# Pooled attention and a ReLU² feed-forward: the first batch pooled on VectorE, the second by accumulating transfers, two hidden blocks begun early

## The chip, the cores and the metric

The kernel runs on one core of a Trainium2 chip. A time is the device time of one execution in microseconds (us). The kernel before has a median of 930.41 us over three runs (928.98 to 931.21).

Engines are called as in the profile: PE is TensorE, DVE VectorE, ACT ScalarE, POOL GpSimd, SP SyncE. SP issues the plain transfers; POOL issues those that add to what lies in the destination ("sums" below).

## The reference, cut to what matters

```python
# q, k, v: [8 batches, 8 heads, 576 tokens, 64]; pool = 8, Sp = 72
k_p = k.reshape(B, H, Sp, pool, D).mean(axis=3)
v_p = v.reshape(B, H, Sp, pool, D).mean(axis=3)
scores = scale * np.matmul(q, k_p.transpose(0, 1, 3, 2))
scores = scores - np.max(scores, axis=-1, keepdims=True)
attn = np.exp(scores)
attn = attn / (np.sum(attn, axis=-1, keepdims=True) + 1e-09)
x = np.matmul(attn, v_p)              # as rows: [4608, 512]
h = np.maximum(x @ w_in, 0.0)         # w_in [512, 2048]
out = h * h @ w_out                   # w_out [2048, 512]
```

## The kernel before, in words

The 4608 token rows are cut into nine chunks of 512. A chunk takes 16 steps, one for each 128 columns of w_in: a *hidden* block (`h`: x times w_in, 128 × 512), ReLU and square on ACT, and, three steps later (LAG), a *project* block (`o`: its product with the rows of w_out, four accumulators kept in PSUM over the chunk). Chunk 0 does both products in plain float32; chunk 1 uses a split in two float32r parts and three products; from chunk 2 on a scheme with seven products takes the place of eight. The attention of a later chunk is done between these blocks, one pair of heads at a time. A chunk has 512 rows and a batch 576, so chunk 1 needs the pooled keys and values of batches 0 and 1, chunk 2 those of batches 1 and 2.

Every engine works strictly in the order in which the code was written. A table `work` says by `at(step, f, ...)` in which step a piece is written; within a step the order is fixed by the loop at the end of the kernel.

The front is the part ahead of step 0: the attention of chunk 0, written out by hand. For every pair of heads it has these stages: pooled keys and the queries are turned by PE (`turn_k`, tile `kps`; `turn_rows`, tile `qps`) and copied by ACT (`kf`, `st`); scores (`token_scores`, tile `sps`), row maximum on DVE (`tm`), exponent on ACT (`te`), division on DVE (`token_normalise`), turned back by PE (`token_turn`, tile `pps`) and copied (`sc`), weighed with the pooled values (`weigh_values`, tile `av`) and copied (`x`). `keep_awake` puts a few idle matmuls (`still`) in front of some of these.

Weights arrive as raw 512 KB tiles (`land`; EAGER = 8 of them are asked for in the front) and are brought to float32 by two ACT instructions (`magnitude`) and three DVE instructions (`to_float32`) each; FIRST tiles are converted in the front, the others in the steps.

Pooling is done in two ways. Batches 0 and 1 arrive whole, a pair of heads to a tile (`load_pair`, 288 KB), and are halved three times by POOL (`by_halves`: three TENSOR_TENSOR per pair); two of the key pairs of batch 0 are reduced by DVE (`reduce_k`). From batch 2 on four heads go to a tile: one plain transfer of 144 KB lays down every eighth-row pair, three accumulating transfers of 144 KB each, issued by POOL, add the others, and `pool` adds the two halves on DVE. A batch has two such tiles for keys and two for values, so 12 accumulating transfers.

SP's transfers take turns on eight semaphores, so an issue waits for the transfer eight before it to land. `dynamic_dma_scratch_size=1024`, the room for POOL's transfers, is the same in both kernels.

Of the kernel before, what the change touches and what calls it, by code (L numbers as in the profile page):

```python
# [37 lines left out]
def pooled_attn_relu2_ffn(  # L38
# [21 lines left out]
    P = 128  # L60
# [18 lines left out]
    FIRST, EAGER, AHEAD = 2, 8, 3  # L79
# [177 lines left out]
    def load_sums(kind, b, n, j):  # L257

        if (kind, b) not in started:
            started.add((kind, b))  # L260
            if kind == "k":
                loaded["kq", b] = sb.tile([SP_, H, D], F32, name=f"kq_{b}", tag="kq", bufs=1)
        src = {"k": k, "v": v}[kind][b].rearrange("h (s j o) d -> j s h (o d)", j=POOL // 2, o=2)[j][:, n * HALF:(n + 1) * HALF]
        if j == 0:
            two[kind, n] = sb.tile([SP_, HALF, 2 * D], F32, name=f"{kind}2_{b}_{n}", tag="two", bufs=2)
            load(two[kind, n], src)
        else:
            GP.dma_start(two[kind, n], src, accum_op=ALU.add)
# [4 lines left out]
    def pool(kind, b, n):  # L273
        new_batch(b)
        dst = kv[b] if kind == "v" else loaded["kq", b]
        t = two.pop((kind, n))
        DVE.tensor_tensor(dst[:, n * HALF:(n + 1) * HALF], t[:, :, :D], t[:, :, D:], op=ALU.add)
        for p in range(n * NPAIR // 2, (n + 1) * NPAIR // 2):
            loaded["kp", b, p] = dst[:, 2 * p:2 * p + 2, :]

    def turn_k(b, pairs=range(NPAIR)):

        pairs = list(pairs)
        pt = (ps_a if b else ps_h).tile([P, 512], F32, name=f"kps_{b}_{pairs[0]}", tag="a" if b else "h")
# [12 lines left out]
        return then  # L297

    def split_k(b, src=None):
        src = kf[b] if src is None else src  # L300
        kh, kl = kk[b] = [sb.tile([P, NPAIR, 2, SP_], F32R, name=f"k{x}_{b}", tag=f"k{x}", bufs=2) for x in "hl"]
        for i, own, oth in heads:
            ACT.copy(kh[own, :, i, :], src[own])
            ACT.copy(kh[oth, :, i, :], src[own])
        for i, own, oth in heads:
            for rows in (own, oth):
                DVE.tensor_tensor(kl[rows, :, i, :], src[own], kh[own, :, i, :].bitcast(F32), op=ALU.subtract)
# [35 lines left out]
    def turn_rows(c, p):  # L343
        src = loaded.pop(("qn", c, p))
        st = live[c, p] = half_tile("s", f"st_{c}_{p}")
        for i, copy in enumerate((ACT.copy, DVE.tensor_copy if p > 1 else ACT.copy)):
            pt = ps_h.tile([P, 512], F32, name=f"qps_{c}_{p}_{i}", tag="h")
            for t in range(NTT):
                PE.transpose(pt[:D, t * P:(t + 1) * P], src[:, i, t, :], ident)
            copy(st[i * D:(i + 1) * D], pt[:D])  # L350
# [81 lines left out]
    def token_scores(c, p):  # L432
# [15 lines left out]
        def then():  # L448
            m = sb.tile([P, 4, 2, NTT], F32, name=f"tm_{c}_{p}", tag="tm", bufs=2)
            e = w_tile(F32, f"te_{c}_{p}")[:, :, :NTT * SP_].rearrange("p i (t n) -> p i t n", t=NTT)  # L450
            e = [e[:, i] for i in range(2)]
            for i in range(2):
                DVE.tensor_reduce(m[:, 0, i], views[i], axis=AX.X, op=ALU.max)
                DVE.tensor_scalar(m[:, 1, i], m[:, 0, i], -SCALE, None, op0=ALU.mult)
            for i in range(2):
                for t in range(NTT):
                    ACT.activation(e[i][:, t], views[i][:, t], AF.Exp, bias=m[:, 1, i, t:t + 1], scale=SCALE)
            live[c, p] = (e, m)
# [3 lines left out]
    def token_normalise(c, p):  # L462
        e, m = live[c, p]
        for i in range(2):
            DVE.tensor_reduce(m[:, 2, i], e[i], axis=AX.X, op=ALU.add)
        DVE.tensor_scalar(m[:, 3], m[:, 2], 1e-9, float(POOL), op0=ALU.add, op1=ALU.mult)
        DVE.reciprocal(m[:, 3], m[:, 3])
        for i in range(2):
            DVE.tensor_tensor(e[i], e[i], m[:, 3, i].unsqueeze(2).to_broadcast([P, NTT, SP_]), op=ALU.mult)
# [20 lines left out]
    def weigh_values(c, p):  # L490
# [4 lines left out]
        av = (ps_h if c < PLAIN else ps_a).tile([P, 512], F32, name=f"av_{c}_{p}", tag="h" if c < PLAIN else "a")  # L495
# [189 lines left out]
    GP.memset(still, 0.0)  # L685
# [55 lines left out]
    token_turn(0, 3)()
    weigh_values(0, 3)()

    for p in range(NPAIR):
        load_pair("k", 1, p)
    for p in range(NPAIR):
        load_pair("v", 1, p)
    issue_loads()
    for p in range(NPAIR):
# [139 lines left out]
```

## Time and profile before

| | us |
|---|---|
| median of three runs (lowest, highest) | 930.41 (928.98, 931.21) |
| the profiled execution, its own time | 927.71 |
| span from its first to its last instruction | 925.9 |
| PE busy / DVE / ACT / POOL | 902.9 / 560.1 / 512.3 / 416.6 |
| mean granted PE clock | 0.990 |

Busy time of PE is modelled from pipelined matmuls, so a PE that is shown busy can still be slowed by what feeds it. All arithmetic goes through one helper line (L34), so a group is known by its tiles, not by its line. In a row of the timeline the first number is the start, the second how long the merged piece lasted, and in brackets stands the idle time ahead of it with what ended it.

### The profile page before, as it was taken

How to read it: one execution, taken by the hardware profiler on the slowest of the kernel's cores; microseconds unless marked ns; L12 is line 12 of the kernel's file. 1: busy time of each engine (PE TensorE's matmuls, PEld its weight loads, DVE VectorE, ACT ScalarE, POOL GpSimd, SP SyncE). 2: the span in 40 equal slices, each digit the busy share in tenths (PEclk: the TensorE clock that was granted, in tenths of full speed). 3: DMA queues.
4: the chain of work that ended last, by engine and by line, in shares of the span. 5: the costliest groups of instructions: out<-in, count | busy, mean ns of one | idle time of the engine just before them, and what ended most of it. 6: DMA issues, size and time to landing. Idle time of an engine off the chain costs nothing.

```text
span 925.9 us, 14226 instructions
## 1 busy us (share of the span) xinstructions
PE 902.9 (98%) x5111; PEld 722.0 (78%) x5114; DVE 560.1 (60%) x971; ACT 512.3 (55%) x1021; POOL 416.6 (45%) x231
## 2 busy tenths in 40 slices
PE   6899999999998999999999999999999999999998
PEld 3444444577777888888888888888888888888987
DVE  3995887476778887555755575657644663353221
ACT  2677657466656655655565556555644564444343
POOL 4752225455544666565666656565444444200000
PEclk7999999999999999999999999999999999999999
DMA  9794655678645555765575557654433353345501
GB/s 253 211 268 95 144 162 155 155 211 223 178 100 162 141 137 118 198 142 135 131 194 137 134 143 182 145 134 127 160 115 115 116 160 104 125 149 178 209 1 46
DMA packets 154231, 138.72 MB, mean 150 GB/s; under 512 B 90360, under 2 KB 119032, under 8 KB 154160
## 3 DMA queue, kind: packets, MB, share of 16 engines
q1 hardware_dynamic: 125360, 127.13, 45.0%
q0 software_dynamic: 28800, 10.68, 10.0%
q8 instruction: 40, 0.66, 0.3%
q14 instruction: 31, 0.25, 0.1%
HBM read 119.65 MB, written 18.06 MB: 149 GB/s over the span
## 4 chain that ended last, share of the span: by engine, by line
PE 85%; DVE 7%; ACT 2%; issue 2%; DMA 2%; SPq 1%; POOL 0%; DVEq 0%; ACTq 0%
PE o L34 40%; PE h L34 37%; PE sps L34 4%; PE av L34 3%; DVE wf_i L34 1%; DVE tm L34 1%; DMA w_o<-kept 1%; DVE gl L34 1%; SPq L34 1%; ACT sc L34 1%; DVE xf L34 1%; DVE st L34 0%; DVE te L34 0%; ACT r L34 0%; DVE vp L34 0%
## 5 line engine op out<-in xcount | busy, mean ns | idle before, releaser
L34 PE MATMUL o<-w_o,gh 128*128 128x512 f32 x1024 | 322.2, 396 | 0.7 <-DMA w_o<-kept 0.5
L34 POOL PARTITION_ALL_REDUCE tot<-sc x56 | 188.8, 3420 | 83.2 <-issue 82.8
L34 PEld LDWEIGHTS o<-w_o,gh 128*128 128x128 f32 x1024 | 184.4, 188 | 45.3 <-issue 7.0
L34 PE MATMUL o<-w_o,gl 128*128 128x512 f32 x512 | 199.6, 390 | 0.0
L34 POOL PARTITION_ALL_REDUCE mx<-sc x56 | 109.3, 1996 | 63.0 <-ACT sc L34 60.7
L34 ACT ACTIVATE r<-h 128x512 f32<-128x512 f32 x144 | 83.5, 595 | 95.9 <-PE h L34 77.5
L34 PE MATMUL h<-x_T,w_S 128*128 128x256 f32 x1008 | 130.6, 283 | 3.6 <-ACT r L34 3.0
L34 PEld LDWEIGHTS h<-x_T,w_S 128*128 128x128 f32 x1008 | 125.1, 192 | 4.2 <-ACT r L34 3.2
L34 PEld LDWEIGHTS o<-w_o,gl 128*128 128x128 f32 x512 | 96.1, 188 | 21.3
L34 DVE TENSOR_TENSOR h<-h,u 128x256 f32<-128x256 f32 x168 | 72.7, 433 | 62.2 <-ACT u L34 33.1
L34 ACT COPY u<-h 128x256 f32<-128x256 f32 x112 | 41.7, 373 | 116.2 <-PE h L34 70.9
L34 PE MATMUL h<-x_B,w_A 128*128 128x256 f32 x672 | 98.5, 283 | 0.4 <-ACT r L34 0.4
L34 PEld LDWEIGHTS h<-x_B,w_A 128*128 128x128 f32 x672 | 91.9, 191 | 5.2 <-ACT r L34 0.8
L34 POOL DMA_DIRECT2D k<-in_k_dram x36 | 44.6, 1239 | 110.8 <-issue 56.2
L34 DVE TENSOR_TENSOR gl<-r,gh 128x512 fp32r<-128x512 f32 x128 | 90.3, 741 | 5.7 <-ACT gh L34 5.6
L34 POOL DMA_DIRECT2D v<-in_v_dram x36 | 44.0, 1223 | 107.1 <-issue 45.4
L34 DVE TENSOR_TENSOR u<-h,u 128x256 f32<-128x256 f32 x56 | 23.4, 418 | 107.9 <-ACT u L34 107.8
L34 ACT ACTIVATE r<-r 128x512 f32<-128x512 f32 x144 | 84.2, 625 | 1.1
L34 DVE TENSOR_TENSOR st<-qs,st 64x512 fp32r<-64x512 f32 x56 | 44.6, 797 | 60.1 <-ACT st L34 59.2
L34 ACT CAST gh<-r 128x512 fp32r<-128x512 f32 x128 | 78.9, 617 | 0.6 <-PE o L34 0.4
L34 ACT ACTIVATE sc<-sc 72x512 f32<-72x512 f32 x56 | 34.5, 632 | 67.0 <-DVE sc L34 67.0
L34 PE MATMUL h<-x,wf_i 128*128 128x512 f32 x128 | 59.4, 609 | 1.9 <-DVE wf_i L34 1.9
(96 smaller groups left out, 1224.1 us busy)
## 6 DMA issues: line engine op xcount, KB each, us to landing
w_o<-kept SPq DMA_DIRECT2D x128, 512.0 KB
out_dram<-ob SPq DMA_DIRECT2D x36, 256.0 KB
raw_i<-in_moe_w_in_dram SPq DMA_DIRECT2D x16, 512.0 KB
raw_o<-in_moe_w_out_dram SPq DMA_DIRECT2D x16, 512.0 KB
kept<-w_o SPq DMA_DIRECT2D x16, 512.0 KB
rb<-rd SPq DMA_DIRECT2D x56, 128.0 KB
k<-in_k_dram POOLq DMA_DIRECT2D x36, 144.0 KB, 5.0
v<-in_v_dram POOLq DMA_DIRECT2D x36, 144.0 KB, 5.3
```

The source lines that it names most:

```text
L34: return lambda *a, **k: self.tc.keep_in_program_order(f(*a, **k))
```

## The change

In the front of chunk 0: DVE reduces three key pairs of batch 0 and POOL one (before: two and two); POOL still halves the values of batch 0. Queries land a pair of heads at a time with the two heads side by side, so that one PE turn of 128 × 128 does both heads and one ACT copy follows (before: two turns of 64 × 128 and two copies). The scale and its sign go into the copy of the pooled keys (`kf`), so the maximum becomes a minimum and the extra multiplication goes. Normalising a pair is one reduction and one multiplication for both heads. Two hidden blocks are begun with each x as it arrives (`begin`). Four weight tiles are converted in the front. The idle tile is cleared by DVE.

Batch 1 arrives by accumulating transfers like the later batches: 4 plain ones of 144 KB and 12 sums. POOL's 24 TENSOR_TENSOR on batch 1 go. The sums of batch 1's keys stand in the front, those of its values in steps 0 to 2, and `pool` on DVE stands in step 2 (keys) and step 5 (values); the turn of batch 1's keys moves from step 1 to step 3. The transfers of batch 2 get a table of their own (NEXT_AT), and their keys are still turned in step 8.

```diff
-    FIRST, EAGER, AHEAD = 2, 8, 3
+    FIRST, EAGER, AHEAD = 4, 8, 3
-    EARLY = ((-15, -12, -10, -7), (0, 1, 2, 3, 4))
+    EARLY = ((-13, -12, -8, -7), (0, 1, 2, 3, 4))
+    NEXT_AT = {"k": ((3, 4, 5, 6, 7), (3, 4, 5, 6, 7)), "v": ((7, 8, 9, 11, 13), (7, 8, 10, 12, 14))}
-    STIR, AWAKE = 10, (2, 3, 3)
+    STIR, AWAKE = 10, (2, 2, 0)
...
-            ACT.copy(kf[b][:, pairs[0]:pairs[-1] + 1, :], turned)
+            ACT.activation(kf[b][:, pairs[0]:pairs[-1] + 1, :], turned, AF.Copy, scale=-SCALE)
...
-    def load_rows(c, j):
+    def load_rows(c, p):
-        t = w_tile(F32, f"qn_{c}_{j}")
...
+        rows = loaded["qn", c, p] = half_tile("qn", f"qn_{c}_{p}").rearrange("p (t h d) -> p t h d", t=NTT, h=2)
+        load(rows, q[0, 2 * p:2 * p + 2, c * CH:(c + 1) * CH, :].rearrange("h (p t) d -> p t h d", t=NTT))
...
+    def begin(cc):
+        for fc in range(2):
+            if cc == 0:
+                begun[fc] = ps_h.tile([P, 512], F32, name=f"h_0_{fc}", tag="h")
+            PE.matmul(begun[fc], lhsT=wf["i", 0, cc // 2, 0][:, cc % 2, fc * P:(fc + 1) * P], rhs=xts[0, cc][:, 0, :],
+                      start=cc == 0, stop=cc == NCC - 1)
...
+    for p in range(NPAIR):
+        load_pair("k", 0, p)
+        load_rows(0, p)
+    load_pair("v", 0, 0)
+    load_pair("v", 0, 1)
+    land(keys[0])
+    load_pair("v", 0, 2)
+    load_pair("v", 0, 3)
+    land(keys[1])
+    for n in range(2):
+        load_sums("k", 1, n, 0)
+    for key in keys[2:EAGER]:
         land(key)
+    for n in range(2):
+        load_sums("v", 1, n, 0)
...
+    for p in range(3):
+        reduce_k(0, p)
+    halve_k(0, 3)
+    more = [(n, j) for j in range(1, POOL // 2) for n in range(2)]
     for p in range(NPAIR):
         halve_v(0, p)
+        if p == 1:
+            load_sums("k", 1, *more.pop(0))
+    for n, j in more:
+        load_sums("k", 1, n, j)
...
-    for p in range(NPAIR):
-        halve_k(1, p)
-    for p in range(NPAIR):
-        halve_v(1, p)
-    at(1, turn_k, 1)
+    v_sums = [(n, j) for j in range(1, POOL // 2) for n in range(2)]
+    for i, (n, j) in enumerate(v_sums):
+        at(i // 2, load_sums, "v", 1, n, j)
+    for n in range(2):
+        at(2, pool, "k", 1, n)
+        at(5, pool, "v", 1, n)
+    at(3, turn_k, 1)
```

Three places show how the change moves instructions. In the names, `k_1` is a key tile of batch 1, `k_2` of batch 2, `v_0_3` the fourth value pair of batch 0; the last number is a buffer's.

POOL after the first value pairs of batch 0, before the change (its last value pair, the first of eight pairs of batch 1, and then, after the eighth, the first sums):

```order
L34 TENSOR_TENSOR v_0_3_86<-v_0_3_86 72x2x256
L34 TENSOR_TENSOR v_0_3_86<-v_0_3_86 72x2x128
L34 TENSOR_TENSOR vp_146<-v_0_3_86 72x128
L34 TENSOR_TENSOR k_1_0_462<-k_1_0_462 72x2x256
L34 TENSOR_TENSOR k_1_0_462<-k_1_0_462 72x2x128
L34 TENSOR_TENSOR kq_478<-k_1_0_462 72x128
```

and with the change (from the end of the second value pair):

```order
L34 TENSOR_TENSOR vp_158<-v_0_1_84 72x128
L34 DMA k_1_90<-in_k_dram 72x4x128
L34 TENSOR_TENSOR v_0_2_86<-v_0_2_86 72x2x256
L34 TENSOR_TENSOR v_0_2_86<-v_0_2_86 72x2x128
L34 TENSOR_TENSOR vp_158<-v_0_2_86 72x128
L34 TENSOR_TENSOR v_0_3_87<-v_0_3_87 72x2x256
L34 TENSOR_TENSOR v_0_3_87<-v_0_3_87 72x2x128
L34 TENSOR_TENSOR vp_158<-v_0_3_87 72x128
L34 DMA k_1_90<-in_k_dram 72x4x128 x5
L34 DMA v_1_97<-in_v_dram 72x4x128 x6
L34 DMA k_2_0_568<-in_k_dram 72x4x128
L34 DMA k_2_1_569<-in_k_dram 72x4x128
```

Twelve sums of batch 1 now stand ahead of batch 2's on the one queue of POOL, and the first of them stands ahead of two value pairs of batch 0.

PE around the turn of batch 1's keys, with the change (`h_3` is the fourth hidden block, `o_0` to `o_3` the four accumulators; the turn stood after `h_1` before):

```order
L34 MATMUL h_3_528<-x_3_428,wf_i_1_389 128x512
L34 MATMUL kps_0_533<-ident,kq_89 128x72 x4
L34 MATMUL o_0_538<-wf_o_440,r_0_459 128x512
L34 MATMUL o_1_539<-wf_o_440,r_0_459 128x512
L34 MATMUL o_2_540<-wf_o_440,r_0_459 128x512
L34 MATMUL o_3_541<-wf_o_440,r_0_459 128x512
L34 MATMUL h_4_572<-x_0_348,wf_i_0_449 128x512
```

All of PE's later work stands behind this turn.

DVE around the addition that ends the pooling of batch 1's keys (`kq`), with the change:

```order
L34 SCALAR_TENSOR_TENSOR wf_o_440<-raw_o_94,wf_o_440 128x512
L34 SCALAR_TENSOR_TENSOR wf_i_0_449<-raw_i_0_0_95,wf_i_0_449 128x2x256
L34 TENSOR_TENSOR kq_89<-k_1_90 72x256 x2
L34 TENSOR_SCALAR wf_i_1_473<-wf_i_1_473 128x2x256
L34 TENSOR_SCALAR wf_o_476<-wf_o_476 128x512
L34 SCALAR_TENSOR_TENSOR wf_i_1_473<-wf_i_1_473,raw_i_1_0_96 128x2x256
```

Half of the weights of block `h_4` (`wf_i_1_473`) are converted behind this addition; before the change POOL made `kq` and DVE had no such instruction for batch 1.

More of the change, by code (lines that the diff above doesn't have):

```diff
@@ L263, in load_sums @@
         src = {"k": k, "v": v}[kind][b].rearrange("h (s j o) d -> j s h (o d)", j=POOL // 2, o=2)[j][:, n * HALF:(n + 1) * HALF]
+        if b < PLAIN:
+            if j == 0 and n == 0:
+                t = w_tile(F32, f"{kind}2_{b}")
+                for i in range(2):
+                    two[kind, b, i] = t[:SP_, i, :].rearrange("s (h x) -> s h x", h=HALF)
+            dst = two[kind, b, n]
+        elif j == 0:
+            dst = two[kind, b, n] = sb.tile([SP_, HALF, 2 * D], F32, name=f"{kind}2_{b}_{n}", tag="two", bufs=2)
+        else:
+            dst = two[kind, b, n]
         if j == 0:
-            two[kind, n] = sb.tile([SP_, HALF, 2 * D], F32, name=f"{kind}2_{b}_{n}", tag="two", bufs=2)
-            load(two[kind, n], src)
+            load(dst, src)
         else:
-            GP.dma_start(two[kind, n], src, accum_op=ALU.add)
+            GP.dma_start(dst, src, accum_op=ALU.add)
     def first_sums(*a):
@@ L302, in split_k @@
         for i, own, oth in heads:
-            ACT.copy(kh[own, :, i, :], src[own])
-            ACT.copy(kh[oth, :, i, :], src[own])
+            ACT.activation(kh[own, :, i, :], src[own], AF.Copy, scale=scale)
+            ACT.activation(kh[oth, :, i, :], src[own], AF.Copy, scale=scale)
         for i, own, oth in heads:
             for rows in (own, oth):
-                DVE.tensor_tensor(kl[rows, :, i, :], src[own], kh[own, :, i, :].bitcast(F32), op=ALU.subtract)
+                DVE.scalar_tensor_tensor(kl[rows, :, i, :], src[own], scale, kh[own, :, i, :].bitcast(F32), op0=ALU.mult, op1=ALU.subtract)
     def segments(c):
@@ L343, in turn_rows @@
     def turn_rows(c, p):
-        src = loaded.pop(("qn", c, p))
+        src = loaded.pop(("qn", c, p)).rearrange("p t h d -> p t (h d)")
         st = live[c, p] = half_tile("s", f"st_{c}_{p}")
[L346 to L350, printed above, removed]
+        pt = ps_h.tile([P, 512], F32, name=f"qps_{c}_{p}", tag="h")
+        for t in range(NTT):
+            PE.transpose(pt[:, t * P:(t + 1) * P], src[:, t], ident)
+        return lambda: ACT.copy(st, pt)
     def transpose_q(c, p):
@@ L448, in then @@
         def then():
-            m = sb.tile([P, 4, 2, NTT], F32, name=f"tm_{c}_{p}", tag="tm", bufs=2)
+            m = sb.tile([P, 3, 2, NTT], F32, name=f"tm_{c}_{p}", tag="tm", bufs=2)
             e = w_tile(F32, f"te_{c}_{p}")[:, :, :NTT * SP_].rearrange("p i (t n) -> p i t n", t=NTT)
-            e = [e[:, i] for i in range(2)]
             for i in range(2):
-                DVE.tensor_reduce(m[:, 0, i], views[i], axis=AX.X, op=ALU.max)
-                DVE.tensor_scalar(m[:, 1, i], m[:, 0, i], -SCALE, None, op0=ALU.mult)
+                DVE.tensor_reduce(m[:, 0, i], views[i], axis=AX.X, op=ALU.min)
             for i in range(2):
                 for t in range(NTT):
-                    ACT.activation(e[i][:, t], views[i][:, t], AF.Exp, bias=m[:, 1, i, t:t + 1], scale=SCALE)
+                    ACT.activation(e[:, i, t], views[i][:, t], AF.Exp, bias=m[:, 0, i, t:t + 1], scale=-1.0)
             live[c, p] = (e, m)
@@ L463, in token_normalise @@
         e, m = live[c, p]
[L464 to L469, printed above, removed]
+        DVE.tensor_reduce(m[:, 1], e, axis=AX.X, op=ALU.add)
+        DVE.tensor_scalar(m[:, 2], m[:, 1], 1e-9, float(POOL), op0=ALU.add, op1=ALU.mult)
+        DVE.reciprocal(m[:, 2], m[:, 2])
+        DVE.tensor_tensor(e, e, m[:, 2].unsqueeze(3).to_broadcast([P, 2, NTT, SP_]), op=ALU.mult)
     def token_turn(c, p):
@@ L678, in pooled_attn_relu2_ffn @@
     first_keys = keys[:FIRST]
-    for key in keys[:EAGER]:
+    for p in range(NPAIR):
[10 more added lines that the diff above has]
+    for key in keys[2:EAGER]:
         land(key)
+    for n in range(2):
+        load_sums("v", 1, n, 0)
     issue_loads()
     still = half_tile("z", "still").bitcast(mybir.dt.bfloat16)
-    GP.memset(still, 0.0)
+    DVE.memset(still, 0.0)
     idle.append(lambda t, n: [PE.matmul(t, lhsT=still[:, :P], rhs=still[:, :512], start=True, stop=True) for _ in range(n)])
@@ new lines, in pooled_attn_relu2_ffn @@
+    for n, j in more:
+        load_sums("k", 1, n, j)
+    st = [None] * NPAIR
+    st[0] = turn_rows(0, 0)
+    kf0 = turn_k(0, [0])
+    st[0](), kf0()
+    exp = [token_scores(0, 0)]
+    st[1] = turn_rows(0, 1)
+    kf1 = turn_k(0, [1])
+    st[1](), kf1()
+    exp[0]()
+    st[2] = turn_rows(0, 2)
+    exp.append(token_scores(0, 1))
+    kf2 = turn_k(0, [2])
+    st[2](), kf2()
+    st[3] = turn_rows(0, 3)
+    st[3]()
+    exp[1]()
+    exp.append(token_scores(0, 2))
+    kf3 = turn_k(0, [3])
@@ L736, in pooled_attn_relu2_ffn @@
+    token_turn(0, 2)()
     weigh_values(0, 1)()
-    token_turn(0, 2)()
+    begin(0)
+    magnitude(keys[1])
+    magnitude(keys[2])
     token_normalise(0, 3)
-    to_float32(*first_keys)
-    weigh_values(0, 2)()
-    token_turn(0, 3)()
-    weigh_values(0, 3)()
-    for p in range(NPAIR):
[L745 to L749, printed above, removed]
-        halve_k(1, p)
-    for p in range(NPAIR):
-        halve_v(1, p)
@@ L753, in pooled_attn_relu2_ffn @@
-    at(1, turn_k, 1)
+    x2 = weigh_values(0, 2)
+    sums = token_turn(0, 3)
+    x2()
+    to_float32(keys[1])
+    begin(1)
+    sums()
+    magnitude(keys[3])
+    weigh_values(0, 3)()
+    begin(2)
+    to_float32(*keys[2:FIRST])
+    begin(3)
+    v_sums = [(n, j) for j in range(1, POOL // 2) for n in range(2)]
[5 more added lines that the diff above has]
+    at(3, turn_k, 1)
@@ L777, in kv_steps @@
             for n in range(2):
+                steps = NEXT_AT[kind][n] if b == PLAIN else [s + start + d for d in HALF_AT[n]]
                 for j in range(POOL // 2):
-                    at(s + start + HALF_AT[n][j], load_sums if j else first_sums, kind, b, n, j)
-                at(s + start + HALF_AT[n][-1], pool, kind, b, n)
-        at(s + KV_AT[1][1] + 3, turn_k, b)
+                    at(steps[j], load_sums if j else first_sums, kind, b, n, j)
+                at(steps[-1], pool, kind, b, n)
+        at(8 if b == PLAIN else s + KV_AT[1][1] + 3, turn_k, b)
     ready = {0, 1}
-    START = {transpose_q: 8, scores: 11}
+    START = {transpose_q: 9, scores: 11}
     stages = (transpose_q, scores, exponents, send_sums, fetch_sums, reciprocals, fetch_reciprocals, weigh_values)
```

66 lines of the change are left out of this document (25 added, 41 removed).

## The prediction

> **What bounds the kernel now.** I read the page's first part, then stretches of time, then each engine's front in order of time.
>
> ```profile
> span 925.9 us, 14226 instructions
> PE 902.9 (98%) x5111; PEld 722.0 (78%) x5114; DVE 560.1 (60%) x971; ACT 512.3 (55%) x1021; POOL 416.6 (45%) x231
> 10.00:20.00 10.00, 4.21 (x25) 3.09 (x26) 3.11 (x6) 0.49 (x3) 6.47 (x8) 0.67 1.05 265
> 20.00:30.00 10.00, 9.53 (x62) 6.54 (x62) 7.07 (x15) 5.79 (x22) 8.08 (x11) 0.65 0.89 327
> 40.00:50.00 10.00, 8.09 (x30) 3.47 (x30) 9.91 (x10) 7.02 (x14) 9.53 (x10) 0.87 0.82 228
> 100.00:165.00 65.00, 64.91 (x211) 29.88 (x211) 52.36 (x93) 45.69 (x93) 22.32 (x13) 1.00 0.54 143
> ```
>
> In a stretch the columns after its length are PE, PEld, DVE, ACT and POOL busy, then PE's clock, the DMA share and GB/s. PE sets the time, and only the first 50 us leave it room: from 100 to 165 us it is busy 64.91 of 65. So where the change puts PE in chunk 0 stays to the end. I compare one place in both kernels: the end of the turn of batch 2's keys, behind hidden block `h_8`.
>
> ```profile
> 15.79 0.50 PE L34 MATMUL kps<-ident,kq 72*128 72x72 f32 x2 [7.05 <-POOL kq L34]
> 47.35 8.80 PE L34 MATMUL h<-x,wf_i 128*128 128x512 f32 x16 [1.85 <-DVE wf_i L34]
> 60.93 3.70 PE L34 MATMUL h<-x,wf_i 128*128 128x512 f32 x8
> 88.27 3.60 PE L34 MATMUL o<-wf_o,r 128*128 128x512 f32 x8
> 91.70 3.60 PE L34 MATMUL h<-x,wf_i 128*128 128x512 f32 x8
> 104.96 0.42 PE L34 MATMUL kps<-ident,kq 72*128 72x72 f32 x4
> 121.14 1.18 PE L34 MATMUL sps<-kf,st 64*64 64x72 f32 x20
> 122.24 1.09 PE L34 MATMUL av<-sc,vp 72*64 72x64 f32 x8
> ```
>
> Before, that place is at 105.4. A block, `h` or `o`, costs 3.43 us from start to start (88.27 to 91.70), a score piece 1.10.
>
> **The front gets shorter, by some 17 us.**
>
> ```profile
> 8.34 1.94 DVE L34 TENSOR_REDUCE kq<-k 72x64 f32<-72x512 f32 x2 [4.75 <-DMA k<-in_k_dram]
> 41.19 2.35 DVE L34 TENSOR_SCALAR wf_i<-wf_i 128x512 f32<-128x512 f32 x2
> 48.00 1.50 DVE L34 TENSOR_SCALAR wf_i<-wf_i 128x512 f32<-128x512 f32 x1
> 88.61 0.42 DVE L34 TENSOR_SCALAR wf_i<-wf_i 128x512 f32<-128x512 f32 x1
> 88.95 0.68 DVE L34 SCALAR_TENSOR_TENSOR wf_o<-wf_o,raw_o 128x512 uint32<-128x512 uint32 x1
> 13.14 2.06 POOL L34 TENSOR_TENSOR k<-k 72x512 f32<-72x512 f32 x2 [11.46 <-issue]
> L34 DVE TENSOR_SCALAR tm<-tm 128x4 f32<-128x4 f32 x8 | 2.6, 322 | 0.3
> L34 DVE COPY st<-qps 64x512 f32<-64x512 f32 x2 | 1.4, 685 | 0.6 <-PE qps L34 0.6
> ```
>
> POOL starts its first addition at 13.14 with nothing shown to wait for, so PE gets its first turned keys at 15.79. DVE reduced a pair by 10.3 (8.34 + 1.94): 5.5 us earlier even if the first pair lands no earlier than the second did. The eight scalings (2.6) and two copies (1.4) leave DVE, which is busy 9.9 of 10 us there; a third reduced pair comes to it (1.9). Converting the first two tiles took 6.8 us (41.19 to 48.00) beside POOL's additions for batch 1; at the later price of 0.33 + 0.60 + 0.60 us a tile it is 3.1, so 3.7 go. Six of the eight matmuls of the first two blocks move into the gaps (6 x 0.86 = 5.1). Sum: 5.5 + 2.6 + 1.4 - 1.9 + 3.7 + 5.1 = 16.4. Before, blocks `h_0` to `h_3` end at 64.6, of which 1.4 are batch 1's turn and scores, which now stand later: 63.2 - 16.4 = 47, where PE reaches the turn of batch 1's keys. Fewer idle matmuls, the minimum for the maximum and the scale in the copy of `kf` I cost at nothing: PE waits there for DVE, and the copy is one instruction as before.
>
> **Batch 1 now goes through POOL's queue of sums.** This decides.
>
> ```profile
> 57.70 1.69 POOL L34 DMA_DIRECT2D k<-in_k_dram  x1
> 65.46 1.22 POOL L34 DMA_DIRECT2D k<-in_k_dram  x1 [6.06 <-DMA q<-in_q_dram]
> 75.31 1.19 POOL L34 DMA_DIRECT2D k<-in_k_dram  x1 [8.63 <-issue]
> 79.49 1.20 POOL L34 DMA_DIRECT2D k<-in_k_dram  x1 [2.99 <-issue]
> 83.78 1.19 POOL L34 DMA_DIRECT2D k<-in_k_dram  x1 [3.09 <-issue]
> 88.16 1.52 POOL L34 DMA_DIRECT2D k<-in_k_dram  x1 [3.19 <-issue]
> 92.75 1.19 POOL L34 DMA_DIRECT2D v<-in_v_dram  x1 [3.08 <-issue]
> k<-in_k_dram POOLq DMA_DIRECT2D x1, 144.0 KB, 7.5
> k<-in_k_dram POOLq DMA_DIRECT2D x1, 144.0 KB, 9.5
> DMA to landing us min/median/max: 3.9/4.2/9.5
> ```
>
> The two single rows are the sums issued at 57.70 and 65.46, with their landing time at the end. The sum at 75.31 goes into the tile of the one at 57.70, landed at 65.2, yet it waited: 65.46 + 9.5 = 74.96 is when the *other* tile's sum landed. At 79.49, 83.78, 88.16 and 92.75 the same. So one sum starts when the one before has landed, whatever its tile: 9.85 us beside weight loads (65.46 to 75.31), 4.42 in quiet (79.49 to 92.75, three), 5.84 over the first six (57.70 to 92.75). Before, 12 sums stand ahead of chunk 2; now 24, and DVE (`pool`), then PE (`kps`), stand in order behind them.
>
> Start. The first sum needs the first plain transfer of batch 1.
>
> ```profile
> 20.87 0.33 SPq L34 DMA_DIRECT2D k<-in_k_dram  x1
> 22.22 1.66 SPq L34 DMA_DIRECT2D k<-in_k_dram  x2
> q1 hardware_dynamic: 1484, 0.26, 63.4%
> q1 hardware_dynamic: 819, 1.06, 92.9%
> ```
>
> SP's issue at 20.87 waited for the first w_in tile, the 11th transfer, with 3,840 KB asked for up to it; the next tile followed 1.35 us later. Now 4,496 KB stand up to batch 1's first transfer: 656/512 x 1.35 = 1.7 later, 22.6. The queries now come in 4,096 pieces of 256 bytes for 1,024 of 1 KB. The queue rows (43 to 46 us, nearly all 128-byte pieces; 2 to 6 us, mostly 1 KB) give 63.4% of 16 engines x 3 us over 1,484 = 20 ns, and 73 ns. So the queries cost 4,096 x 20/16 = 5.2 us for 4.7 before, up to 18.7: start between 23 and 37. I take 25, near the low end, since 256 bytes are nearer to 128.
>
> First gate: 25 + 7.5 (it runs beside weight loads; two value pairs halved by POOL hide in it, 5.2 us) + 5 x 5.84 = 61.7, then two additions of 0.42 and the turn: 62.8. PE, there at 47, waits 16 us. The whole gain of the front goes into this wait: at 64.6 before, PE had done the same four blocks and the scores (1.10) besides.
>
> Second gate: the six sums of values, at 5.13 (the middle of 5.84 and 4.42, as the weight loads thin out): 92.5. DVE adds them in step 5 ahead of normalising chunk 1's first pair, which PE turns after `h_6`.
>
> ```profile
> 87.94 0.42 DVE L34 TENSOR_TENSOR kq<-k 72x256 f32<-72x256 f32 x1 [3.80 <-DMA k<-in_k_dram]
> 93.22 0.81 DVE L34 TENSOR_REDUCE tm<-te 128x4 f32<-128x288 f32 x2
> 94.51 0.83 DVE L34 TENSOR_TENSOR te<-te,tm 128x288 f32<-128x288 f32 x2
> ```
>
> PE's own way there is six blocks and two score pieces, 22.8: it arrives at 85.6. Additions 0.8 and normalising 2.0 (93.22 to 95.25) let it go at 95.3: a second wait, 10 us.
>
> Third gate: the six key sums of batch 2 at 4.42, quiet since SP's loads wait for tiles that a waiting PE and DVE do not free: 92.5 + 26.5 = 119.0; additions and turn: 120.1. PE's own way from 95.3 is four blocks, two turns back (0.87 each) and one `av` (1.02): 16.5, so 112.
>
> Sum: 120.1 - 105.4 = 14.7, and by this place the new order has one score piece (1.10) less behind it: 15.8. From here PE is full in both. Batch 2's values follow at 119 + 6 x 4.42 = 146; step 14 wants them, six steps of two blocks (6.86) behind the third gate, 161. Profiled execution: 927.71 + 15.8 = 943.5. The runs' median lies 2.7 above that execution (930.41), so 946.2.
>
> Bounds of the price: with s = 25 the third gate is 33.6 + 17p for a mean distance p. At the least cadence seen, 4.18 (75.31 to 79.49), it is 104.7: no difference. At 5.84 throughout it is 132.9, 28.6 us later. PE's clock fell after its idle 7.05 us (0.67 and 0.65 in the rows above); after the first two waits the next gate takes that up, after the third, some 8 us, it can cost up to 3; I take nothing.
>
> The Trainium skill (TensorE: Matmul & The Clock Gate, "Part 1: The HAM clock gate") says that about 3.4 us of idle halve the clock and about 3.4 us of work restore it; this case's trace agrees with the first. By it my estimate would be 1.7 us longer.
>
> **Rivals.**
>
> *Sums that do not hold PE: faster.* If two sums were in flight, or one cost under 4.2, the gates would open ahead of PE, at the sums' own place in the queue, and the front's gain would stay. With half of 5.84 the third gate is 25 + 6.4 + 17 x 2.92 = 81; PE's own way from 47 (22.8 + 16.5 + 0.3) ends at 87, 18 earlier than before. DVE and ACT, busy 52 and 46 of 65 us there, must convert the weights that much sooner, which may cost up to 8 of it: 10 to 18 us faster. I take 12: 930.4 - 12 = 918. For: the two halves of a tile are independent. Against: all seven issues above.
>
> The Trainium skill (DMA: Bandwidth & Descriptors, "Anatomy of one DMA — SWDGE (gpsimd) path") fits such a transfer as 2.0 us + bytes/436e3, here 2.3 us. By it this rival would hold; the rows disagree, none is below 3.9.
>
> *No difference.* The quiet cadence from the start: 930. Against: the first sums run beside the same weight loads as those of 57.70 and 65.46.
>
> *Heavier.* 5.84 throughout, or queries that land late: 930.4 + 28.6 = 959.
>
> *The front does not get shorter* (late queries, or the value pairs behind the first sum). It changes nothing up to 16 us: the first gate stands at 62.8 all the same. Not a case of its own.
>
> **How the numbers follow.** Forecast (waits at the gates, 938 to 955 for the mixed prices): 0.56. Heavier: 0.18. No difference, within 0.2% (1.9 us, about what a measurement can tell): 0.09. Faster: 0.17. Slower is 0.56 + 0.18 = 0.74. Predicted 946. A range from 924 to 960 leaves out most of the faster case (0.11) and the end of the heavier one (0.06).
>
> **What would show it.** Right: the sums of batch 1 and 2 as a chain, each starting within 0.4 us of its predecessor's landing; PE idle ahead of `kps` near 47 to 62, ahead of the first `pps` of chunk 1 near 86 to 95, and DVE idle until `k` and `v` transfers; `kps` of batch 2 ending near 120; the first `x` times `w_in` before 35. Wrong: sums closer than 3.9 us, or `kps` of batch 2 ending before 105; or idle time after 165 us in the kernel before that the new order uses better, for which I saw none.

## The result, and the profile after

The changed kernel takes 964.3 us (four runs, 960.6 to 973.1), the kernel before 930.8 in the same comparison (928.98 to 931.34). The ratio is 1.0377, 95% interval 1.0302 to 1.0452: 33.5 us slower. The direction is the one predicted; 946 was 18 us too little, and the time lies above the range (924 to 960). The medians below leave out one execution, of the kernel with 39 buffers, which took 1608.9 us at a mean clock of 0.776.

The profiled execution took 962.24 us. Its first part, and the group of plain project blocks:

```profile
span 960.5 us, 14101 instructions
PE 904.6 (94%) x5082; PEld 719.8 (75%) x5082; DVE 559.5 (58%) x944; ACT 511.9 (53%) x1019; POOL 405.1 (42%) x215
L34 PE MATMUL o<-wf_o,r 128*128 128x512 f32 x128 | 64.3, 650 | 0.0
```

The same group before (x128 in both; the mean granted clock is 0.974 after and 0.990 before):

```profile
L34 PE MATMUL o<-wf_o,r 128*128 128x512 f32 x128 | 58.2, 597 | 0.0
```

PE has hardly more to do (904.6 us busy for 902.9) in a span 34.6 us longer. The project blocks of chunks 0 and 1 (`o<-wf_o`) alone took 6.1 us more, so the rest of PE's work took 4.4 less (5082 instructions for 5111). Where PE stood still is seen in its order of time (start, length, and in brackets the idle time ahead and what ended it):

```profile
40.44 7.13 PE L34 MATMUL h<-x,wf_i 128*128 128x512 f32 x16 [1.00 <-ACT r L34]
...
68.40 0.47 PE L34 MATMUL kps<-ident,kq 72*128 72x72 f32 x2 [20.83 <-DVE kq L34]
72.54 0.50 PE L34 MATMUL kps<-ident,kq 72*128 72x72 f32 x2 [3.67 <-DVE kq L34]
72.84 6.32 PE L34 MATMUL o<-wf_o,r 128*128 128x512 f32 x8
...
105.26 1.89 PE L34 MATMUL pps<-ident,te 128*72 128x128 f32 x8 [6.33 <-DVE te L34]
...
129.52 0.50 PE L34 MATMUL kps<-ident,kq 72*128 72x72 f32 x2 [4.80 <-DVE kq L34]
131.85 5.86 PE L34 MATMUL o<-wf_o,r 128*128 128x512 f32 x8
```

Three gates, as forecast: the turn of batch 1's keys (20.83 + 3.67 us idle), the turning back of chunk 1's first pair (6.33), the turn of batch 2's keys (4.80, and 0.47 for its first half). What opens them is the chain of POOL's sums, and DVE behind it:

```profile
24.03 1.52 POOL L34 DMA_DIRECT2D k<-in_k_dram  x1 [2.49 <-DMA k<-in_k_dram]
...
32.85 1.29 POOL L34 DMA_DIRECT2D k<-in_k_dram  x1 [1.00 <-issue]
41.98 1.19 POOL L34 DMA_DIRECT2D k<-in_k_dram  x1 [7.84 <-issue]
48.83 1.20 POOL L34 DMA_DIRECT2D k<-in_k_dram  x1 [5.66 <-issue]
61.26 1.19 POOL L34 DMA_DIRECT2D k<-in_k_dram  x1 [11.23 <-issue]
68.05 1.20 POOL L34 DMA_DIRECT2D k<-in_k_dram  x1 [5.60 <-issue]
72.35 1.45 POOL L34 DMA_DIRECT2D v<-in_v_dram  x1 [3.10 <-issue]
...
103.08 1.19 POOL L34 DMA_DIRECT2D k<-in_k_dram  x1 [2.92 <-issue]
...
129.33 1.45 POOL L34 DMA_DIRECT2D v<-in_v_dram  x1 [4.02 <-issue]
67.83 0.42 DVE L34 TENSOR_TENSOR kq<-k 72x256 f32<-72x256 f32 x1 [25.62 <-DMA k<-in_k_dram]
```

Every sum stands alone: from 32.85 on each comes 4 to 12 us after the one before, with nothing else for POOL to do. The first five land 8.6, 8.8, 6.5, 12.1 and 6.5 us after their start, and the next one starts within 0.4 us of that, as the prediction had it. Place by place:

| | predicted | measured |
|---|---|---|
| PE reaches the turn of batch 1's keys | 47 | 47.6 (40.44 + 7.13) |
| first sum starts | 25 | 24.03 |
| six key sums of batch 1 | 36.7 | 48.3 (24.03 to 72.35) |
| first gate: turn ended | 62.8 | 73.0 |
| six value sums of batch 1 | 30.8 | 30.7 (72.35 to 103.08) |
| second gate: PE goes on | 95.3 | 105.3 |
| six key sums of batch 2 | 26.5 | 26.3 (103.08 to 129.33) |
| third gate: turn ended (before: 105.4) | 120.1 | 130.0 |
| what comes behind it, against before | +1.1 | +10.0 |

The last row is the span's difference, 960.5 - 925.9 = 34.6, less the 24.6 of the third gate.

### The profile page after: what moved, and what is told of

The parts are those of the page before. It is cut to its first block, busy times and chain, and to the rows that moved or that the text cites. A ratio compares the mean times of both kernels' runs of the same rounds, so it can differ in the third digit from the quotient of the medians.

```text
span 960.5 us, 14101 instructions
## 1 busy us (share of the span) xinstructions
PE 904.6 (94%) x5082; PEld 719.8 (75%) x5082; DVE 559.5 (58%) x944; ACT 511.9 (53%) x1019; POOL 405.1 (42%) x215
## 4 chain that ended last, share of the span: by engine, by line
PE 69%; issue 9%; DVE 9%; DMA 6%; ACT 3%; POOL 3%; SPq 1%; DVEq 0%; ACTq 0%; POOLq 0%
PE o L34 34%; PE h L34 30%; DMA k<-in_k_dram 3%; PE sps L34 3%; PE av L34 2%; DMA w_o<-kept 2%; DVE wf_i L34 1%; POOL k L34 1%; POOL v L34 1%; DVE gl L34 1%; DVE xf L34 1%; DVE wf_o L34 1%; DVE st L34 1%; DMA rb<-rd 1%; ACT sc L34 1%
## 5 line engine op out<-in xcount | busy, mean ns | idle before, releaser
L34 POOL DMA_DIRECT2D k<-in_k_dram x42 | 51.4, 1223 | 141.4 <-issue 91.7
L34 POOL DMA_DIRECT2D v<-in_v_dram x42 | 51.7, 1230 | 133.3 <-issue 57.0
L34 DVE TENSOR_TENSOR gl<-r,gh 128x512 fp32r<-128x512 f32 x128 | 94.4, 773 | 6.0 <-ACT gh L34 5.9
L34 PE MATMUL o<-wf_o,r 128*128 128x512 f32 x128 | 64.3, 650 | 0.0
```

What stands on the lines that cost most here:

```text
L34: return lambda *a, **k: self.tc.keep_in_program_order(f(*a, **k))
```

## The experiments

The theory: batch 1's twelve sums, one under way at a time, hold DVE and through it PE, and the front's gain is lost in the first wait. The rivals: another part of the front or of the tables costs the time; or sums and front both count. Times stand as medians; ratios are to the kernel before on the same chip.

### The sums without the new front, and the front without the sums

The first kernel is the one before with its own front and only batch 1's way changed (`load_sums` for batches below PLAIN, POOL's 24 additions taken out, `pool`, `turn_k` and the tables as in the changed kernel):

```diff
-    for p in range(NPAIR):
-        halve_k(1, p)
-    for p in range(NPAIR):
-        halve_v(1, p)
-    at(1, turn_k, 1)
...
+    for n in range(2):
+        at(2, pool, "k", 1, n)
+        at(5, pool, "v", 1, n)
+    at(3, turn_k, 1)
```

> The kernel before with its own front, and only batch 1 by sums (with the table for batch 2 and the places of the pooling and turning as in the changed kernel). Theory: the end of the chain of sums sets the end and not PE, so that the old front loses nothing by being longer: batch 2's keys are turned at 122 to 136 as in the changed kernel (130), time 955 to 970. Rival 1 (the new front is what costs): 925 to 935. Rival 2 (front and sums both count): 975 to 985, the changed kernel's time and the 16 us of the front.

Measured: 960.9 us (959.4 to 963.0), ratio 1.0319 (1.0292 to 1.0347). PE of that kernel:

```profile
69.48 0.50 PE L34 MATMUL kps<-ident,kq 72*128 72x72 f32 x2 [10.68 <-DVE kq L34]
...
104.09 1.89 PE L34 MATMUL pps<-ident,te 128*72 128x128 f32 x8 [3.82 <-DVE te L34]
...
128.86 0.50 PE L34 MATMUL kps<-ident,kq 72*128 72x72 f32 x2 [3.93 <-DVE kq L34]
```

The gates stand where the changed kernel has them (the last turn of batch 1 ends at 74 for 73, PE goes on at 104.1 for 105.3, the last turn of batch 2 ends at 129.4 for 130.0), though its front is the old, longer one: PE only waits less (10.68 for 20.83) ahead of the first. So the sums alone bring the loss, and the new front buys nothing behind them. The second kernel is the changed one without the twelve sums (its batch 1 is pooled over two rows of every eight):

```diff
-            GP.dma_start(dst, src, accum_op=ALU.add)
+            if b >= PLAIN:
+                GP.dma_start(dst, src, accum_op=ALU.add)
```

> The changed kernel without the twelve sums of batch 1: its keys and values hold only the first two rows of every eight, everything else stands. Theory (the sums, one behind the other, hold PE at three gates): PE is at the turn of batch 1's keys near 47.6 and goes on at once; batch 2's six key sums start near 48 to 52 and end 26 to 48 us later, about when PE has its six blocks behind it (88 to 92); batch 2's keys are turned by 85 to 100 where the changed kernel turned them at 130; the time is 912 to 928. Rival 1 (something else of the change costs the time: 256-byte pieces, begun blocks, fewer idle matmuls): above 945. Rival 2 (batch 2's sums alone already hold PE): 930 to 945.

Measured: 925.8 us (923.7 to 929.2), ratio 0.9944 (0.9920 to 0.9969).

```profile
48.47 0.42 PE L34 MATMUL kps<-ident,kq 72*128 72x72 f32 x4
...
90.99 0.34 PE L34 MATMUL kps<-ident,kq 72*128 72x72 f32 x2 [2.02 <-DVE kq L34]
```

No gate at batch 1, and batch 2's keys turned by 91.3, as the theory has it. PE's own way from 48.5 to 88.7 is what the prediction had for it (22.8 + 16.5). But 14 us earlier at that place are 5.7 at the end (931.5 - 925.8): something behind the gates costs time here too, although PE hardly waits at them.

### One sum at a time: the room

Four times the room for POOL's transfers; there was no memory left for it, so one of the 40 buffers of the weights' pool went. A second kernel gives up the buffer alone.

```diff
-    SLOTS, STREAM, LD = 40, 1, 2
+    SLOTS, STREAM, LD = 39, 1, 2
...
-    nc = _bacc.Bacc("TRN2", target_bir_lowering=False, num_devices=1, dynamic_dma_scratch_size=1024)
+    nc = _bacc.Bacc("TRN2", target_bir_lowering=False, num_devices=1, dynamic_dma_scratch_size=4096)
```

> The changed kernel with four times the room for POOL's transfers (4096 for 1024); one of the 40 buffers of the weights' pool goes for it (39). Theory A (the room lets one sum be under way at a time): several sums are under way together, starts in the chain come closer than 3 us, the first gate opens before 60 and the later ones before PE arrives; time 915 to 935. Theory B (sums stand one behind the other for another reason, such as their order on the queue): each sum still starts when the one before has landed; time 960 to 970. If the buffer that is gone holds weights up, 5 us more in both.

> The changed kernel with 39 buffers in the weights' pool instead of 40 and the room for POOL's transfers as it is: what the kernel with four times the room gave up. That one turned batch 2's keys at 106.7 instead of 130.0 and still took 974.3. Theory (the buffer costs it, each later chunk 4 to 8 us longer by waits for the kept w_out tiles, and the room by itself gains): 980 to 1005 here, 15 to 30 above the kernel with the room. Rival (two sums under way at a time cost later what they gain): 962 to 972.

Measured: with room and 39 buffers 974.3 us, ratio 1.0463 (1.0431 to 1.0495); with 39 buffers alone 1000.4, ratio 1.0744 (1.0687 to 1.0801). POOL and PE with the room, in order of time, and then PE's waits by cause (total, times, longest):

```profile
75.14 3.03 POOL L34 DMA_DIRECT2D k<-in_k_dram  x2
81.70 2.42 POOL L34 DMA_DIRECT2D k<-in_k_dram  x2 [3.53 <-DMA k<-in_k_dram]
106.31 0.42 PE L34 MATMUL kps<-ident,kq 72*128 72x72 f32 x4
```

```profile
PE o L34 <- DMA w_o<-kept: 22.9, 20, 3.0
```

With the buffer gone and the room as it was, the same two views:

```profile
131.18 0.50 PE L34 MATMUL kps<-ident,kq 72*128 72x72 f32 x2 [4.31 <-DVE kq L34]
```

```profile
PE o L34 <- DMA w_o<-kept: 21.9, 22, 2.6
```

The `x2` rows are two sums issued together: the room of 1024 was what let only one be under way (theory A). With two at a time the six key sums of batch 1 are issued in 26.5 us and its six value sums in 23.1 (they begin at 25.50 and 52.02, batch 2's at 75.14), where the changed kernel took 48.3 and 30.7. PE still waits 14.8 us at batch 1's keys (4.95 + 9.89; their turn ends at 63.7, not before 60 as expected), and not at all at batch 2's. The room brings batch 2's keys from 131.2 to 106.3 and the whole kernel from 1000.4 to 974.3. The time expected for theory A, 915 to 935, was missed, because the buffer costs some 36 us (1000.4 for 964.3): both kernels wait 22 us for the kept w_out tiles, where the changed kernel waited 1.7. The other 16 of the 36 I did not part. A pair took 6.6 us (75.14 to 81.70) beside a printed DMA share of 1.33, which is 3.3 a sum; single sums near full engines took some 7 to 12 (next section).

### Why the first six cost 8.0 us and not 5.84

In this kernel chunk 1's first queries wait for POOL, which writes a column of their tiles behind the six key sums. SP stands behind them with all later weights: it issues nothing from 30.2 to 55.1.

```diff
-            qt = sb.tile([P, CH], F32, name=f"q_{c}_{p}", tag="ld", bufs=LD)
+            qt = held[p] if c == 1 and p < 2 else sb.tile([P, CH], F32, name=f"q_{c}_{p}", tag="ld", bufs=LD)
...
     for n, j in more:
         load_sums("k", 1, n, j)
+    held = {}
+    for p in range(2):
+        held[p] = sb.tile([P, CH], F32, name=f"q_1_{p}", tag="ld", bufs=LD)
+        GP.memset(held[p][:, :1], 0.0)
```

> The changed kernel, in which the queries of chunk 1's first two pairs wait until POOL has issued the six key sums of batch 1 (POOL writes one column of their tiles behind the sums), so that SP holds these queries and every weight tile behind them. Theory (a sum costs 8.0 us on the mean there because weights and 128-byte query pieces go beside it): the first six take 33 to 41 us instead of 48.3, the first gate opens at 58 to 66 instead of 72.8; the traffic that was held then goes beside the six value sums, 36 to 45 us instead of 30.7, so the third gate ends at 122 to 130 and the time is 952 to 965. Rival (the price has nothing to do with what goes beside): the first six again 46 to 50 us, and 964 to 975, since the queries come later.

Measured: 963.75 us (959.1 to 966.0), ratio 1.0352 (1.0314 to 1.0390). By stretches between two sums, first this kernel (length, then PE, PEld, DVE, ACT, POOL busy, PE's clock, DMA share, GB/s):

```profile
24.27:40.88 16.61, 16.04 (x69) 6.99 (x68) 14.61 (x25) 13.72 (x31) 8.91 (x8) 1.00 0.92 282
40.88:58.19 17.31, 7.61 (x18) 3.19 (x18) 2.94 (x6) 7.75 (x14) 4.93 (x6) 0.81 0.32 38
58.19:98.95 40.76, 25.34 (x90) 11.66 (x90) 12.47 (x26) 14.52 (x35) 6.22 (x5) 0.79 0.92 230
```

The changed kernel:

```profile
24.03:48.83 24.80, 20.74 (x68) 8.28 (x64) 17.27 (x25) 20.70 (x43) 9.99 (x10) 1.00 0.98 256
48.83:61.26 12.43, 0.00 (x0) 0.00 (x0) 0.00 (x0) 0.00 (x0) 1.20 (x2) 0.58 1.02 270
72.35:103.08 30.73, 26.39 (x90) 12.03 (x90) 12.90 (x27) 14.07 (x35) 7.42 (x6) 0.89 0.58 115
103.08:129.33 26.25, 18.98 (x58) 9.14 (x58) 13.45 (x28) 11.30 (x21) 7.16 (x7) 0.89 0.32 40
```

The kernel before:

```profile
57.70:75.31 17.61, 17.61 (x66) 8.49 (x65) 17.16 (x37) 14.47 (x32) 2.92 (x4) 1.00 0.87 235
75.31:92.75 17.44, 17.44 (x65) 7.93 (x64) 6.62 (x15) 11.90 (x28) 5.10 (x4) 1.00 0.39 53
```

Each stretch holds whole sums, so its length by their number is the price of one:

| stretch | sums | DMA share | us a sum |
|---|---|---|---|
| held, 40.88 to 58.19 | 4 | 0.32 | 4.3 |
| after, 103.08 to 129.33 | 6 | 0.32 | 4.4 |
| before, 75.31 to 92.75 | 4 | 0.39 | 4.4 |
| after, 72.35 to 103.08 | 6 | 0.58 | 5.1 |
| after, 61.26 to 72.35 | 2 | 0.54 | 5.5 |
| before, 57.70 to 75.31 | 2 | 0.87 | 8.8 |
| held, 58.19 to 98.95 | 5 | 0.92 | 8.2 |
| held, 24.27 to 40.88 | 2 | 0.92 | 8.3 |
| after, 24.03 to 48.83 | 3 | 0.98 | 8.3 |
| after, 48.83 to 61.26 | 1 | 1.02 | 12.4 |

The price follows what else the DMA engines carry: about 4.4 us at a third (from 103.08 to 129.33 the sums themselves are 0.30 of the 0.32), and 8 to 9 in the mean of most stretches near full. It is no fixed figure there: single sums took from 6.7 us (88.11 to 94.77, share 0.86) to 12.4 (48.83 to 61.26). With the queries held, the first six take 33.9 us (24.27 to 58.19) and the first gate opens at 58.9 instead of 73.0; the six value sums then meet the traffic (44.9 us, to 103.06), and PE waits at the second gate:

```profile
58.38 0.50 PE L34 MATMUL kps<-ident,kq 72*128 72x72 f32 x2 [3.83 <-DVE kq L34]
...
105.24 1.89 PE L34 MATMUL pps<-ident,te 128*72 128x128 f32 x8 [21.51 <-DVE te L34]
...
129.41 0.50 PE L34 MATMUL kps<-ident,kq 72*128 72x72 f32 x2 [4.72 <-DVE kq L34]
```

The third gate stays at 130, as expected: the traffic has to pass some sums or others. The Trainium skill (SBUF — State Buffer, "SBUF: two separate sides") has another cause ready: transfers issued by GpSimd can stall while VectorE runs an operation that holds the ports the two share. In the stretch with the dearest sum (48.83 to 61.26) DVE was busy 0.00 us, so that is not what made it 12.4.

### Batch 1 by POOL's additions, and the tables by themselves

Two kernels keep the new front and have POOL halve batch 1 as before (keys land behind the fourth weight tile, values behind the sixth): one with the changed tables, one with the old ones. A third is the kernel before with the changed tables alone.

```diff
+    for p in range(NPAIR):
+        load_pair("k", 1, p)
...
+    for p in range(NPAIR):
+        halve_k(1, p)
+    for p in range(NPAIR):
+        halve_v(1, p)
```

> The changed kernel with batch 1 pooled by additions on POOL as before (24 instructions, whole pairs of heads loaded behind the fourth weight tile), turned in step 3. Theory: no gate is left; PE reaches the turn of batch 1's keys near 50 and goes through; POOL is done with batch 1 near 47 to 55, batch 2's keys are turned at 90 to 100; time 912 to 926. Against a full gain speak POOL's additions beside DVE's conversions (up to 4 us). Rival 1 (another part of the change costs): above 945. Rival 2 (DVE beside POOL takes the front's gain back): 926 to 934.

> The front alone: the changed kernel's front, with batch 1 pooled by POOL's additions and every table of the later steps as before (batch 1's keys turned in step 1). It differs from the run with additions (938.8) only by these tables. Theory (the tables put batch 2's sums and chunk 1's scores later, and that is what cost there): batch 2's keys turned by 94 to 101 instead of 104, and 914 to 926. Rival (POOL's additions beside DVE take the front's gain back, the tables do nothing): 934 to 942.

> The kernel before with only the changed tables (chunk 1's pairs, batch 2's sums, the turn of batch 1's keys in step 3). All kernels with these tables took 119 to 120 us from the turn of batch 2's keys to that of batch 3's, the kernel before 113.9. Theory 1 (the order of the tables costs these 5 to 6 us): 118 or more here as well, 934 to 942. Theory 2 (the score piece more, 1.1, and what an idle PE leaves behind, its low clock): 114 to 116 here, 929 to 935.

Measured: with the changed tables 938.75 us, ratio 1.0068 (1.0033 to 1.0102); with the old ones 940.2, ratio 1.0109 (1.0078 to 1.0140); the tables alone 931.8, ratio 1.0019 (1.0002 to 1.0035). My theory missed in both kernels with additions: the front's gain was not there to keep. With the changed tables PE also waits 3.48 + 5.51 us for batch 2's keys, which are turned by 104.0. PE and DVE of the one with the old tables:

```profile
45.43 0.38 PE L34 MATMUL kps<-ident,kq 72*128 72x72 f32 x1 [3.11 <-POOL kq L34]
50.27 5.49 PE L34 MATMUL h<-x,wf_i 128*128 128x512 f32 x8 [4.46 <-ACT r L34]
...
60.88 3.60 PE L34 MATMUL o<-wf_o,r 128*128 128x512 f32 x8
89.39 0.42 DVE L34 TENSOR_TENSOR kq<-k 72x256 f32<-72x256 f32 x1 [9.05 <-DMA k<-in_k_dram]
96.84 1.92 PE L34 MATMUL pps<-ident,te 128*72 128x128 f32 x8 [5.13 <-DVE te L34]
```

PE starts its first project block at 60.88, 3.6 us earlier than before (64.47), where the front had promised 16: it waits for POOL's additions of batch 1 (3.11 us at the last keys), then 4.46 for ACT's relu of an earlier block. And batch 2's six key sums, at their old places, are in by 89.4 (DVE idle 9.05 ahead of its addition), and what stands behind that on DVE lets PE wait 5.13: the sums of batch 2 alone, which before ended just in time (3.80 idle on DVE at 87.94, none on PE), hold up a front that is faster than the old one. In these two kernels POOL's additions beside DVE and the late sums both count; I did not part them further.

The tables alone cost 1.2 us. In that kernel, with no wait at the turn of batch 2's keys, it is 117.1 us from there to the same place of batch 3 (103.19 to 220.30; before: 104.96 to 218.81, 113.9; the changed kernel 129.52 to 249.28, 119.8). So of the changed kernel's 5.9 more, 3.2 are the order of the tables and 2.7 what a PE that waited leaves behind. These are single executions, but the kernel with wide sums for both batches (next section), which has the same tables and no wait at that turn, takes 117.0 as well (89.09 to 206.11). Of the 3.2, 1.1 are the score piece, and 1.0 is a wait of PE for DVE's `x` (at 152.42) that the kernel before does not have. The 117.1 lies between the two expectations (118 or more; 114 to 116); the time, 931.8, is the second one's (929 to 935).

### Fewer and wider sums

If a sum costs nearly the same whatever it carries, fewer of them must help. Four rows of every eight lie side by side instead of two: 4 sums of 288 KB a batch instead of 12 of 144 KB, and one more addition on DVE for each tile (0.68 us). The diff is that for batches 1 and 2; for batch 1 alone the condition is `b < PLAIN`.

```diff
-        src = ....rearrange("h (s j o) d -> j s h (o d)", j=POOL // 2, o=2)[j][:, n * HALF:(n + 1) * HALF]
+        wide = 4 if b <= PLAIN else 2
+        src = ....rearrange("h (s j o) d -> j s h (o d)", j=POOL // wide, o=wide)[j][:, n * HALF:(n + 1) * HALF]
...
+        if b <= PLAIN:
+            DVE.tensor_tensor(t[:, :, :2 * D], t[:, :, :2 * D], t[:, :, 2 * D:], op=ALU.add)
```

> The changed kernel with batch 1 pooled by 4 sums of 288 KB in place of 12 of 144 KB (four rows of every eight lie side by side instead of two, the same number of pieces, each 1 KB; DVE adds twice instead of once, about 4 us more). Theory (the chain of sums, each with a mostly fixed price, sets the gates): first two sums 16 to 20 us, in by 45; values in by 60; batch 2's six key sums end at 85 to 95, no gate holds PE for more than 3 us; time 920 to 931. Rival (the price goes with the bytes): a sum takes 14 us or more beside the loads, the chain is hardly shorter, 945 to 964.

> As the kernel with four sums of 288 KB for batch 1 (936.9), and batch 2 in four such sums as well: two for its keys in place of six, two for its values in place of six. There the six key sums of batch 2 ran from 70.49 to 102 and held PE 12.2 us. Theory (the chain of sums sets the third gate): two sums, 8 to 10 us each, end by 91; PE, whose own way ends near 89, waits less than 4 us; its clock stays at 1.00 there; batch 2's keys are turned by 89 to 94 instead of 103.5; 918 to 928, below the kernel before. Rival (what is lost behind the turn of batch 2's keys, 8 to 13 us in every kernel with these tables, eats it whatever the gate does): 929 to 935.

Measured: batch 1 alone 936.9 us (933.9 to 941.3), ratio 1.0072 (1.0049 to 1.0095); both batches 921.6 (918.8 to 924.4), ratio 0.9892 (0.9861 to 0.9924). The first:

```profile
70.49 1.19 POOL L34 DMA_DIRECT2D k<-in_k_dram  x1 [11.49 <-issue]
...
103.09 0.50 PE L34 MATMUL kps<-ident,kq 72*128 72x72 f32 x2 [4.70 <-DVE kq L34]
```

The first gate is gone (0.27 us idle at 50.12), but the six narrow key sums of batch 2 start at 70.49 and still hold PE until 103.6; 920 to 931 was too good. With batch 2 wide too:

```profile
25.45 1.52 POOL L34 DMA_DIRECT2D k<-in_k_dram  x1 [3.54 <-DMA k<-in_k_dram]
...
35.71 1.23 POOL L34 DMA_DIRECT2D k<-in_k_dram  x1 [2.26 <-issue]
48.05 1.68 POOL L34 DMA_DIRECT2D v<-in_v_dram  x1 [11.11 <-DMA q<-in_q_dram]
56.32 1.20 POOL L34 DMA_DIRECT2D v<-in_v_dram  x1 [6.59 <-DMA q<-in_q_dram]
69.69 1.19 POOL L34 DMA_DIRECT2D k<-in_k_dram  x1 [12.17 <-DMA k<-in_k_dram]
79.16 1.20 POOL L34 DMA_DIRECT2D k<-in_k_dram  x1 [8.28 <-DMA q<-in_q_dram]
...
89.09 0.42 PE L34 MATMUL kps<-ident,kq 72*128 72x72 f32 x4
```

From one wide sum to the next it is 10.3 us (POOL's value pairs between), 12.3, 8.3 and, from 69.69, 9.5, beside DMA shares of 0.84 to 0.99. Single narrow ones near full engines took 6.7 to 12.4, so the bytes count for little there, and there are a third as many sums. Behind 93 us, at shares of 0.59 and 0.68, two wide ones landed after 5.6 and 5.4 us. PE turns batch 2's keys at 89.09 without a wait. This version beats both kernels: 9.2 us below the one before (930.8), some 43 below the changed one.

## Why the prediction came out as it did

**Right.** These came as forecast: the front's shortening (PE reaches the turn of batch 1's keys at 47 predicted, 47.6 measured) and that it is worth nothing at the first gate; the chain of single sums; the kind and order of all three gates, though each opened some 10 us late; the time of the last twelve sums (30.8 and 26.5 predicted, 30.7 and 26.3 measured); and PE's own way of 40 us between the first and the third gate, which the kernel without the sums shows. The 30.8 was in part luck: its price of 5.13 was the middle of two figures, and the six sums took 4.1 to 7.0 us each. The kernel without the front, at nearly the same time, confirms that the gates set the end. For gates that open ahead of PE the rival "sums that do not hold PE" had named 918; 921.6 came, by fewer sums and not by its two sums in flight or a price under 4.2.

**Right for partly wrong reasons.** Inside the front the terms were off and cancelled. The first turned keys came at 6.57, 9.2 us earlier and not 5.5, since the first pair lands well before DVE's first reduction of the old order. The 3.7 us for the first weight tiles did not come: POOL's value pairs still run beside them, and one instruction there took 3.14 us. The 2.1 us that leave DVE in sum do not show on PE either: from its first scores (7.54 for 17.07) to its last `av` (34.73 for 44.23) the lead stays at 9.5 us. That the total was off by less than 1 us is luck.

```profile
6.57 0.23 PE L34 MATMUL kps<-ident,kq 72*128 72x72 f32 x1
24.29 3.14 DVE L34 SCALAR_TENSOR_TENSOR wf_i<-wf_i,raw_i 128x512 uint32<-128x512 uint32 x1
```

**Wrong: the price of the first six sums (5.84).** It was the mean of six sums of the kernel before, of which two ran beside nearly full DMA engines (share 0.87) and four in quiet (0.39). In the changed kernel the first four ran beside a DMA share near one, because nothing held SP: while PE and DVE stood, SP still sent for chunk 1's queries and for weight tiles that found free buffers, the last at 55.19. The step "SP's loads wait for tiles that a waiting PE and DVE do not free" was right for the last six (share 0.32) and was not asked of the first six. They took 48.3 us for 36.7, and that error, 11.6 us less 1.0 for the earlier start, stands almost unchanged at the third gate: 130.0 for 120.1, 9.9 us. The mean over all 18 sums, (129.33 - 24.03) / 18 = 5.85, is the number of the rival "heavier" (5.84 throughout, third gate at 132.9, chance 0.18).

**Wrong: "from here PE is full in both".** Behind the third gate the changed kernel loses 10.0 us, of which 1.1 was counted. To the turn of batch 3's keys it is 5.9: 3.2 from the order and 2.7 from the wait, by the tables alone. The wait's part is the clock, which the prediction priced at "up to 3" and took as nothing: it stands at 0.50 from 129.5 to about 136.2, so `av` at 129.95 takes 1.98 us for 1.09, and `o` at 131.85 takes 5.86, where it takes 3.60 otherwise, some 3.2 us in the two rows, a little more than the 2.7. The Trainium skill (TensorE: Matmul & The Clock Gate, "Part 1: The HAM clock gate") gave 1.7 us for it by its rule of about 3.4 us; the trace agrees that such an idle time halves the clock, but the half clock lasted about 6.7 us here, twice as long. The last 4.1 us, behind batch 3's keys, stay open. The gates are not their cause: from that turn to the end of the span the kernel before takes 706.7 us, the changed one 710.8, and the one with wide sums for both batches, which hardly waits at any gate, 710.5. PE's waits for kept w_out tiles grew from 0.5 to 1.7 us; the profiled execution of the kernel before lies 2.7 below its median, and executions of the changed kernel differ by 12.5 us among themselves.

In sum: 946.2 + 9.9 (first six sums) + 4.8 (order and clock, beyond the 1.1) + 4.1 (open) - 0.6 (the median lies 2.1 above the profiled execution, not 2.7) = 964.4.

## What to carry to other kernels

A chain of transfers that can only run one at a time is an engine of its own: add up its links from the first to the consumer, and give each link the price of the traffic that will stand beside it there, not the mean of another place. When such a chain bounds the end, shortening the work ahead of it is worth nothing, moving the traffic only changes which link pays, and fewer, wider links helped most here. And a stalled consumer does not make the queues quiet: ask what still frees or holds the engine that issues the loads.

## What the runs showed of the hardware

- A 144 KB sum took 4.3 us in the mean at a DMA share of 0.32, and single ones took 6.7 to 12.4 at shares of 0.83 to 1.04. Sums of twice the bytes followed one another by 8.3 to 12.3 at 0.84 to 0.99.
- The room for POOL's transfers decides how many of them are under way: with 1024 one, with 4096 two together, at 6.6 us for two (75.14 to 81.70).
- One weight buffer fewer of 40 cost 36 us. 22 us of PE's waits for the kept w_out tiles are seen (1.7 with 40), 2.6 at the most each, spread over every later chunk.
- After PE's wait of 4.80 us at the third gate its clock stood at 0.50 for about 6.7 us.
